# A spectral filter and a gated network on one core: other gates and queues for the opening's loads, two steps' shift of batch 1, and x chunks in whole-width transfers

## The chip, the cores and the metric

The kernel runs on one core of a Trainium2 chip. The metric is the device time of one execution in microseconds (us), the median over the runs; less is better. The profile is of one execution, taken by the hardware profiler. Engines are named as in it: PE is TensorE, DVE is VectorE, ACT is ScalarE, POOL is GpSimd, SP is SyncE. Three of them issue transfers here: SP, ACT and POOL, each in the order of its own program; the profile calls SP's queue q1, ACT's q10 and POOL's q0.

## The reference

`x` has 8 batches of 3008 positions by 256 channels, float32. Each batch is filtered in the frequency domain along its positions, and the result goes through a gated network:

```python
X = np.fft.rfft(x, axis=1)
Y = X * (filt_r + 1j * filt_i)[None, :, :]
y = np.fft.irfft(Y, n=x.shape[1], axis=1)      # (8, 3008, 256)

t = y.reshape(8 * 3008, 256)
gate = np.maximum(t @ w_gate, 0.0)             # (256, 1536)
val = t @ w_val                                # (256, 1536)
out = (gate * val) @ w_out                     # (1536, 256)
```

## The kernel before, in words

A position is written as 32 n1 + n2, with 94 values of n1 and 32 of n2, and the transform of 3008 points is done as matrix products of two levels.

**A** transforms along n1. For batches 0 and 1 this is `first_a` (fp32 products `psA`, evicted by ACT at L289), and `turn_a` on DVE (L301) brings the result into the layout `at`. Batch 0's pieces come first, batch 1's sixteen follow through the iterator `early`. For batches 2 to 7, `load_chunk` brings x in four chunks per batch into the tiles `XP`, `fold_chunk` adds and subtracts them on POOL, `tiled_a` multiplies (`psF`) and stores to `Abuf` in DRAM through SP, and `load_at_tiled` reads `at` back through SP (L355).

**B** has six parts per batch: `fwd` transforms along n2 (`psX`), `product` multiplies with the filters on DVE (`tt`, `uu`), `inv` transforms back (`psD`, evicted into `dsb`) and stores to `Dbuf` in DRAM through SP (L422). Batch 0's last store uses the tile `AS[0][0]` again, which appears as `AS` in `Dbuf<-AS`.

**D** reads `Dbuf` back: `load_d` (L448) makes four tiles `dC` per batch (z = 0 to 3, eight values of n2 each), each with two transfers of 192 KB.

**C** is `item_c`: the last product along n1 for a block of 512 tokens (`psY`, L471), copied to `yT` by ACT for one half and by DVE for the other.

**The network** then takes the 47 blocks of 512 tokens in 12 feature tiles each. `gv` (L487) makes `psV` and `psG`; ACT copies V (`vsb`, L490) and DVE multiplies (`prod`, L492). `o_part` (L508) multiplies the previous block's products with `WoT` and the result goes out through `osb` (L521, L532).

The order of all engines is written out by hand. The opening does A and B of batch 0 with nothing beside them, and the A of batch 1; in between, the last transfers and weights are loaded. After that, one loop over blocks and feature tiles runs, with step number 12 x block + tile. At each step it calls `gv`, then a piece of `o_part`, then whatever `at_step` has put on this step: pieces of A and B of later batches, loads of x and of D. `item_c` for the next block stands at tiles 8 and 10. For batch 1, `end` is step 51; its D is first needed by `item_c` at step 56, where the fifth block runs over from batch 0 into batch 1.

Weights are loaded by POOL, since the transfer also casts to bf16: V and G in two halves each (`load_vg`, the first half has tiles 0 to 5), then `WoT` in two (`load_o`). POOL is kept back by small reads of a tile: `hold_gpsimd` copies eight values of it and so waits until it has been written. POOL's instructions behind such a read wait with it. In the opening, before:

- POOL waits for an eviction of batch 1's A (L274), then issues the first halves of V and G;
- SP issues D's reads for z = 0 and 1, as soon as batch 0's last store has landed;
- POOL waits for the z = 0 tile, then issues the second halves of V and G, `WoT`, and D's reads for z = 2 and 3;
- at step 2, POOL clears the four `XP` tiles (L623), since a chunk's 24-row loads leave rows of 32 unwritten.

The memory of the opening's tiles (the pool `pro`) is given back for the loop's tiles (the pool `fs`).

## Time and profile before

| | us |
|---|---|
| median of 3 runs | 889.26 |
| lowest, highest | 887.65, 892.39 |
| profiled execution, its own time | 888.4 |
| profiled execution, span | 886.3 |
| PE busy | 863.7 (97%) |
| DVE busy | 573.8 (65%) |
| ACT busy | 500.7 (56%) |
| POOL busy | 373.5 (42%) |
| granted TensorE clock, mean | 0.999 |

The span is from the first to the last instruction in the trace; the execution's time has 2.1 us around it. The profile moved 104.41 MB in 105731 packets by DMA, 118 GB/s on average. Matmuls are pipelined, so a busy PE is one with work in it. The waits of PE add up over the whole span; the chain of waits follows the work that ended last back from the end, and says for each piece what released it.

### The profile page before, as it was taken

How to read it: one execution, taken by the hardware profiler on the slowest of the kernel's cores; microseconds unless marked ns; L12 is line 12 of the kernel's file. 1: busy time of each engine (PE TensorE's matmuls, PEld its weight loads, DVE VectorE, ACT ScalarE, POOL GpSimd, SP SyncE). 2: the span in 40 equal slices, each digit the busy share in tenths (PEclk: the TensorE clock that was granted, in tenths of full speed). 3: DMA queues.
4: the chain of work that ended last, by engine and by line, in shares of the span. 5: the costliest groups of instructions: out<-in, count | busy, mean ns of one | idle time of the engine just before them, and what ended most of it. 6: DMA issues, size and time to landing. Idle time of an engine off the chain costs nothing.

```text
span 886.3 us, 19058 instructions
## 1 busy us (share of the span) xinstructions
PE 863.7 (97%) x7071; PEld 508.0 (57%) x7193; DVE 573.8 (65%) x863; ACT 500.7 (56%) x905; POOL 373.5 (42%) x374
## 2 busy tenths in 40 slices
PE   8989999999999999999999999999999999999998
PEld 4336555566556665566655565556655556566665
DVE  3768765577666776667765676657776577655553
ACT  4765554555655565556565556555655555555553
POOL 6661795137641567316771167802867000000001
PEclk9999999999999999999999999999999999999999
DMA  9992466533466337543375234753446512321111
GB/s 238 282 177 49 137 155 139 133 101 113 116 155 137 102 102 165 130 112 101 105 190 131 81 100 129 182 118 84 118 133 150 123 31 81 91 65 36 38 31 54
DMA packets 105731, 104.41 MB, mean 118 GB/s; under 512 B 20215, under 2 KB 90391, under 8 KB 104966
## 3 DMA queue, kind: packets, MB, share of 16 engines
q1 hardware_dynamic: 82374, 75.21, 33.3%
q0 software_dynamic: 22864, 27.19, 13.1%
q8 instruction: 57, 0.93, 0.5%
q10 hardware_dynamic: 400, 0.79, 0.3%
q14 instruction: 36, 0.29, 0.1%
HBM read 58.93 MB, written 46.66 MB: 119 GB/s over the span
## 4 chain that ended last, share of the span: by engine, by line
PE 85%; DMA 7%; DVE 2%; ACT 2%; issue 1%; POOL 1%; SPq 1%; POOLq 0%; DVEq 0%
PE psG L487 26%; PE psO L508 25%; PE psV L487 24%; PE psF L337 3%; PE psD L411 2%; PE psY L471 2%; DVE prod L492 2%; PE psX L374 2%; ACT vsb L490 2%; DMA dC<-Dbuf 2%; DMA at<-Abuf 1%; DMA XF<-in_x_dram 1%; DMA Fti<-in_filt_i_dram 1%; DMA Fti<-Fti 1%; DMA Dbuf<-dsb 1%
## 5 line engine op out<-in xcount | busy, mean ns | idle before, releaser
L492 DVE SCALAR_TENSOR_TENSOR prod<-psG,vsb 128x512 bf16<-128x512 f32 x564 | 388.7, 690 | 259.6 <-ACT vsb L490 253.2
L490 ACT CAST vsb<-psV 128x512 bf16<-128x512 f32 x564 | 331.9, 589 | 265.5 <-PE psV L487 137.4
L508 PE MATMUL psO<-WoT,prod 128*128 128x256 bf16 x2256 | 336.5, 273 | 1.1
L487 PE MATMUL psG<-yT,WgT 128*128 128x512 bf16 x1105 | 330.4, 379 | 5.8 <-DMA WgT<-in_moe_w_gate_dram 0.6
L487 PE MATMUL psV<-yT,WvT 128*128 128x512 bf16 x1031 | 315.9, 380 | 1.2 <-DVE yT L478 0.7
L508 PEld LDWEIGHTS <-prod 128*128 128x128 bf16 x2256 | 220.7, 98 | 143.3
L487 PEld LDWEIGHTS <-WgT 128*128 128x128 bf16 x1128 | 110.0, 98 | 135.6 <-issue 1.8
L487 PEld LDWEIGHTS <-WvT 128*128 128x128 bf16 x1128 | 98.3, 98 | 40.7 <-issue 29.5
L274 POOL CAST scr<-prod 128x8 f32<-128x8 bf16 x24 | 4.5, 190 | 254.7 <-DVE prod L492 254.7
L532 POOL DMA_DIRECT2D out_dram<-osb x5 | 2.6, 535 | 195.7 <-ACT osb L521 195.7
L521 ACT COPY osb<-psO 128x512 f32<-128x512 f32 x92 | 53.9, 586 | 25.8 <-PE psO L508 24.6
L390 DVE TENSOR_TENSOR tt<-psX,Ftr 128x512 bf16<-128x512 f32 x96 | 64.9, 681 | 1.6 <-PE psX L374 0.9
L323 POOL TENSOR_TENSOR fold<-XP 128x1024 f32<-128x1024 f32 x24 | 56.5, 2355 | 19.5 <-PE psF L337 19.3
L390 DVE TENSOR_TENSOR uu<-psX,Fti 128x512 bf16<-128x512 f32 x88 | 59.8, 680 | 0.0
L310 POOL DMA_DIRECT2D XP<-in_x_dram x96 | 56.6, 593 | 2.8 <-PE psY L471 1.4
L324 POOL TENSOR_TENSOR XP<-XP 128x1024 f32<-128x1024 f32 x24 | 56.4, 2349 | 1.9
L419 ACT CAST dsb<-psD 128x512 bf16<-128x512 f32 x94 | 50.6, 592 | 11.0 <-PE psD L411 11.0
L344 ACT CAST asb<-psF 128x512 bf16<-128x512 f32 x48 | 25.8, 589 | 30.1 <-PE psF L337 30.1
L344 DVE CAST asb<-psF 128x512 bf16<-128x512 f32 x48 | 30.9, 686 | 18.1 <-PE psF L337 17.3
L476 ACT CAST yT<-psY 128x512 bf16<-128x512 f32 x47 | 27.5, 586 | 26.1 <-PE psY L471 25.9
L471 PE MATMUL psY<-M,dC 96*128 96x94 bf16 (+18 forms) x604 | 37.7, 198 | 3.6 <-DMA dC<-Dbuf 3.6
L471 PEld LDWEIGHTS <-dC 96*128 96x128 bf16 x604 | 34.4, 97 | 7.9 <-issue 3.4
(73 smaller groups left out, 503.0 us busy)
## 6 DMA issues: line engine op xcount, KB each, us to landing
XP<-in_x_dram POOLq DMA_DIRECT2D x48, 256.0 KB, 6.0
Dbuf<-dsb SPq DMA_DIRECT2D x23, 512.0 KB
dC<-Dbuf SPq DMA_DIRECT2D x60, 192.0 KB
XP<-in_x_dram POOLq DMA_DIRECT2D x96, 96.0 KB, 2.7
Abuf<-asb SPq DMA_DIRECT2D x96, 96.0 KB
at<-Abuf SPq DMA_DIRECT2D x24, 384.0 KB
out_dram<-osb SPq DMA_DIRECT2D x69, 94.0 KB
XF<-in_x_dram SPq DMA_DIRECT2D x20, 256.0 KB
```

The costliest lines, as they stand in the source:

```text
L310: nc.gpsimd.dma_start(xp[r:r + 24, 0:4:2, :], _ap(x, (b * N1 * N2 + o) * D, [[N2 * D, 24], [47 * N2 * D, 2], [1, 512]]))
L323: tt(t, xp[:, 0:2], xp[:, 2:4], op=ALU.add)
L324: tt(xp[:, 2:4], xp[:, 0:2], xp[:, 2:4], op=ALU.subtract)
L344: copy(asf[:, :, q, :], banks[q])
L390: nc.vector.tensor_tensor(p, psX, filt, op=ALU.mult)
L419: copy(dsb[:, a, o:o + 2, :], psD[a])
L471: nc.tensor.matmul(psY[:, o:o + w], dCs[b, n2 // 8][:, n2 % 8, h * 128:(h + 1) * 128], M1[:, n1:n1 + w], start=True, stop=True)
L487: nc.tensor.matmul(pt[:, :W], w[:, h, ft * 128:(ft + 1) * 128], yt[:, h, :], start=(h == 0), stop=(h == 1))
L490: nc.scalar.copy(vsb, psV[:, :W])
L492: nc.vector.scalar_tensor_tensor(prod, in0=psG[:, :W], scalar=0.0, in1=vsb, op0=ALU.max, op1=ALU.mult)
L508: nc.tensor.matmul(psO[:, t % 2], prods[ft][:, t * 128:(t + 1) * 128], WoT[:, ft, :], start=(ft == 0), stop=(ft == NFT - 1))
L521: copy(osb[:, t0 % 2:t % 2 + 1], psO[:, t0 % 2:t % 2 + 1])
```

## The change

- In the opening, six pieces of batch 1's A (three before) stand ahead of the loads. POOL's gate becomes a memset of a few values of `AS[0][0]`, which has to wait until batch 0's last store has read that tile. Behind it, both halves of V and G and `WoT` are issued with no second gate.
- D's read for z = 0 is issued half on SP and half on ACT; z = 1 stays on SP, z = 2 and 3 on POOL.
- The first of the last four `turn_a` pieces of batch 1 moves from step 5 to the end of the opening; the other three go from steps 11, 14, 16 to 6, 12, 14.
- Batch 1's B goes two steps earlier, its D reads one step (50 to 49). The chunks of batch 2 go from steps 22, 29, 34, 43 to 14, 23, 32, 41.
- A chunk is loaded by four transfers of 128 partitions, 256 KB each, in place of four of 96 KB and two of 256 KB; the rows that no product reads now hold other rows of x, and the clearing is gone.

```diff
 def load_chunk(b, j):
     xp = XP[j]
-    for q in range(4):
-        r, o = 32 * q, 8 * q + 2 * j
-        nc.gpsimd.dma_start(xp[r:r + 24, 0:4:2, :],
-                          _ap(x, (b * N1 * N2 + o) * D,
-                              [[N2 * D, 24], [47 * N2 * D, 2], [1, 512]]))
-    for i in range(2):
-        nc.gpsimd.dma_start(xp[:, 2 * i + 1, :],
-                          _ap(x, ((b * N1 + 46 + 47 * i) * N2 + 2 * j) * D,
-                              [[8 * D, 4], [-N2 * D, 32], [1, 512]]))
+    for i in range(4):
+        up = N2 * D if i % 2 == 0 else -N2 * D
+        nc.gpsimd.dma_start(xp[:, i, :],
+                            _ap(x, ((b * N1 + 46 * (i % 2) + 47 * (i // 2)) * N2 + 2 * j) * D,
+                                [[8 * D, 4], [up, 32], [1, 512]]))
...
 first_b(amid)
-for _ in range(3):
-    p, s, h = next(early)
-    first_a(1, p, s, h)
-hold_gpsimd(AS[2][0][:, 4 * s, p, 0:8])
+for _ in range(6):
+    first_a(1, *next(early))
+nc.gpsimd.memset(AS[0][0][:, 0, 0, 0:8], 0.0)
 load_vg(0, DFF // 2)
-load_d(0, 0, 2)
-hold_gpsimd(dCs[0, 0][:, 7, D - 8:])
 load_vg(DFF // 2, DFF)
 load_o()
+load_d(0, 0, 1, (nc.sync, nc.scalar))
+load_d(0, 1, 2)
 load_d(0, 2, 4, (nc.gpsimd, nc.gpsimd))
...
 for h in range(2):
     item_c(0, h)
+turn_a(1, 1, 0, 0, 16)
...
-def clear_chunks():
+def make_chunks():
     for i in range(4):
         XP.append(fs.tile([128, 4, 512], FP32, tag=f"XP{i}", bufs=1, name=f"XP{i}"))
-        nc.gpsimd.memset(XP[i], 0.0)
...
-for k in range(4):
-    at_step((5, 11, 14, 16)[k], lambda k=k: turn_a(1, 1, k // 2, k % 2 * 16, k % 2 * 16 + 16))
-at_step(2, clear_chunks)
+for k in range(1, 4):
+    at_step((6, 12, 14)[k - 1], lambda k=k: turn_a(1, 1, k // 2, k % 2 * 16, k % 2 * 16 + 16))
+at_step(2, make_chunks)
...
-                l = (22, 29, 34, 43)[j] if b == 2 else end - 115 + NFT * j
+                l = (14, 23, 32, 41)[j] if b == 2 else end - 115 + NFT * j
...
-        l = -33 + 5 * i if b == 1 else -40 + 6 * i
+        l = -35 + 5 * i if b == 1 else -40 + 6 * i
...
-    at_step(end - (1 if b == 1 else 2), lambda b=b: load_d(b))
+    at_step(end - 2, lambda b=b: load_d(b))
```

## The prediction

> **What bounds the kernel now.** I read the page first: span, busy time, DMA load over the span.

> ```profile
> span 886.3 us, 19058 instructions
> ...
> PE 863.7 (97%) x7071; PEld 508.0 (57%) x7193; DVE 573.8 (65%) x863; ACT 500.7 (56%) x905; POOL 373.5 (42%) x374
> ...
> DMA  9992466533466337543375234753446512321111
> ```

> TensorE (PE) is busy for 863.7 of 886.3 us, so no scheduling change can win more than 22.6 us, some of it in the first copies and the tail, which this change leaves alone. The DMA digits show where transfers are scarce: the first three slices (66 us), full or nearly. Next, what PE waited for over the whole run.

> ```profile
> PE psY L471 <- DMA dC<-Dbuf: 3.6, 2, 1.9
> ...
> PE psX L374 <- DMA at<-Abuf: 0.8, 1, 0.8
> PE psV L487 <- DVE yT L478: 0.7, 2, 0.4
> PE psG L487 <- DMA WgT<-in_moe_w_gate_dram: 0.6, 1, 0.6
> ```

> Columns: total us, times, longest. The same question for 180 to 800 us returns no row: the steady part has nothing to win. The two psY waits are 1.8 us in the opening and 1.9 us at batch 1's D. The chain of waits shows both, the opening first (start, length, what).

> ```profile
> 40.43 4.99 DMA Dbuf<-AS
> ...
> 45.48 0.33 SPq L448
> ...
> 45.86 6.76 DMA dC<-Dbuf
> ...
> 53.90 6.42 DMA WgT<-in_moe_w_gate_dram
> ...
> 60.37 0.61 PE psG L487 x2
> ```

> D's last store of batch 0 lands at 45.42, its first read at 52.63, and only then do the second halves of V and G leave; PE stops for G's second half until 60.37. The DMA queues between 45.5 and 49.4 us say why the read was slow (queue, packets, MB, share of the 16 engines):

> ```profile
> q0 software_dynamic: 467, 0.69, 108.7%
> ```

> q0 is POOL's queue, with the first halves of V and G. Not one packet of the read, issued on SP (q1) at 45.48, moved in those 3.9 us. From 49.4 to 52.7 us it is the other way:

> ```profile
> q1 hardware_dynamic: 1343, 0.66, 109.1%
> q0 software_dynamic: 57, 0.06, 11.0%
> ```

> POOL's timeline has the issues, and the clearing that goes:

> ```profile
> 43.34 0.78 POOL L262 DMA_DIRECT2D WvT<-in_moe_w_val_dram  x1
> 44.11 0.71 POOL L262 DMA_DIRECT2D WgT<-in_moe_w_gate_dram  x1
> ...
> 58.74 7.09 POOL L623 MEMSET XP<- 128x2048 f32 x4
> ```

> Last, batch 1's D in the chain, and two rows of ACT's timeline:

> ```profile
> 123.09 6.49 DMA Dbuf<-dsb
> ...
> 130.01 6.74 DMA dC<-Dbuf
> ...
> 136.89 0.19 PE psY L471
> ```

> ```profile
> 45.02 0.58 ACT L289 CAST AS<-psA 128x512 bf16<-128x512 f32 x1 [0.27 <-PE psA L282]
> ...
> 51.03 0.65 ACT L289 CAST asb<-psA 128x256 bf16<-128x256 f32 x2 [0.21 <-PE psA L282]
> ```

> **Opening: when D's first read lands.** The memset waits for the store (45.42), then V's issue follows. Before, the hold at 43.10 led to the issue at 43.34, and q0's first packet came at 44.8, 1.4 after the issue. So the first weight packet moves from 44.8 to about 45.5 + 0.2 + 1.4 = 47.1. The read issues at 45.48 on SP; batch 2's read, issued into idle queues at 239.46, starts moving after 1.0 us, so packets flow from 46.5, ahead of the weights. The other half is on ACT, behind the sixth eviction (45.02 + 0.58 = 45.60) and the same store; ACT's issues of x take 0.5 to 0.6 us each and the tail's first one moved packets 0.8 after its issue: 46.4 to 46.7. This issue makes ACT about 0.5 late, and seven evictions are queued behind it; each leaves 0.21 to 0.27 idle and banks are spare, so PE does not see it. In the old run the four 192 KB reads (and WF) took 49.4 to about 54.0, with G's end beside them, some 4.2 us, 0.95 each. Two in front: z = 0 lands at 46.5 + 1.9 + 0.3 = 48.7, before 52.63 and before PE is free. PE's last psA ends at 51.03, so psY starts there, 1.73 us earlier than 52.76; ACT's last eviction (to 51.7), the yT copies (0.6 and 0.7) put psV at 52.4 instead of 53.83.

> **Opening: the weights become late.** Before, they used the DMA engines from 44.8; now these idle until 46.5, and D's reads are first. V's second half was issued at 53.20, G's landed at 60.32: 1.4 to start, about 1.5 extra for ramp and landing, 2.1 for each load. From 46.5: reads 4.2, V and G 4.2 gives 54.9; if the z = 1 reads come later, 53.0. I take 54.7, as the SP issues of z = 1 (46.0 and 46.4, plus 1.0) reach the engines about when V does. So psG starts at 54.7, not 54.38: the 1.8 us wait for dC comes back as a wait for WgT. The second halves now follow without a gap: G's lands at 54.9 + 4.2 = 59.1. Six feature tiles after the first psG took 60.37 - 54.38 - 0.64 = 5.35, so the seventh psG is due at 60.05 and finds its weights: 0.3 earlier than 60.37. With the better order it is 59.1: 1.3 earlier. I take a gain of 0.5. Bounds: all weights in time, 1.4 + 0.64, about 2.1 gained; reads and weights taking turns packet by packet (768 packets of the read at 0.043 us, each behind a weight packet of 0.14, over 16 engines: 8.8 us from 46.7, so z = 0 lands at 55.5 and psG follows at 56.9), 2.5 lost. WoT: 59.1 + 5.5 (its old distance behind G: 65.83 - 60.32) = 64.6; first needed about 66. D's z = 2 and 3 on POOL wait for V and G to land, and are needed after 70.

> DVE's extra transpose (1.21) comes behind yT and ends about 53.9, before the first psG; the piece at step 5 goes to step 6, and one leaves the end of block 0: cost nothing, gain at most the 0.3 us psV wait at 66.22, not counted.

> **Batch 1's D.** B starts two steps earlier. A step is psV, psG, psO: 0.43 + 0.43 + 0.44 = 1.30. The store goes from 123.09 to 120.5, and if store and read keep 6.49 and 6.74, the read lands 2.6 us earlier, at 134.15; PE asked for it at 135.02. The wait of 1.87 is gone even so. Cover on top: the chunk loads, at 121.9 to 125.6 beside this store, move to about 112 (steps 43 to 41, and POOL no longer late by its folds); D's read goes in front of chunk 0's Abuf store (125.99), both on SP, because step 49 lists it first; the Abuf data are not read before 162. Next late is at<-Abuf (0.8 at 176), fed by steps that do not move. Gain 1.9; bounds 0 (if the earlier B work meets DVE at a yT copy and loses as much: that row cost 0.4) and 2.3.

> **Chunks.** Per chunk POOL loses 4 x 0.586 + 2 x 0.702 = 3.75 and gets 4 x 0.702 = 2.81: 22.5 us less over 24 chunks, and 7.1 of memset. No PE row in 180 to 800 waits for POOL or a chunk: worth 0. Bytes rise from 896 to 1024 KB, 3.1 MB of 104.4, where half the DMA time is idle: 0, except at 172 to 176, where a chunk lands beside at<-Abuf: -0.8 to +0.8, taken as 0.

> **Sum.** -0.5 - 1.9 + 0 = -2.4. The profiled run took 888.4 (span 886.3 and 2.1 around it), giving 886.0; the median of the runs shown, 889.26, is 0.9 above it, giving 886.9.

> [...] From 45.5 to 49.4 q0 moved 467 packets and the waiting read none: whoever has work in the engines first keeps them, as far as this row goes. [...] The other: the gap from 51.03 to 52.76, without a busy PE, left the granted clock at 1.00. [...]

> **Rivals.** (1) Slower: the ACT half of the read arrives after the first weight packet (47.1) and, as the read did at 45.5, gets nothing until POOL's queue runs dry: four weights at 2.1 and two WoT loads at 2.75 end at 61.1, the half lands about 62, psY starts 9.3 us late, the G stall of 0.64 and batch 1's 1.9 are saved: +6.8, 896. For: the 3.9 us without a packet. Against: ACT is free at 45.60 and needs to start before about 46.2. Chance 0.10. (2) No gain: the weights' new wait costs 2 and cancels batch 1's gain: 889.3. Chance 0.15. (3) The opening wins its 2.1, batch 1 1.9 and the at wait 0.8: -4.8, 884.5. Against: the DMA digits at 9. Chance 0.15. The forecast has 0.60.

> **Numbers.** 0.5%, about what a measurement of this kernel can tell from no change, is 4.4 us: lines at 884.8 and 893.7. Below 884.8 lie 0.11 of (3) and 0.07 of the forecast (runs spread by 4.7 us): 0.18. Above 893.7: (1) and 0.02 of (2): 0.12. The range, 884.0 to 891.0, takes in (2), (3) and leaves out (1) and the ends.

> **What would show it.** Right: psY near 51.0, psV near 52.4, psG waiting for WgT until 54 to 55, no stall at the seventh psG, no psY wait near 135, at<-Abuf unchanged. Wrong: dC landing after 51, q10 without packets while q0 moves, a granted clock under 1.00 near 55, or new PE rows after 180.

## The result, and the profile after

The changed kernel took 893.06 us (median of 14 runs, 888.30 to 896.10). The kernel before took 888.23 on the same chips (14 runs, 885.38 to 892.39). The ratio, after to before, is 1.0046 with an interval of 1.0028 to 1.0064: slower, by about the size that a measurement of this kernel can tell. The forecast was 886.9, with a range of 884.0 to 891.0 and a chance of 0.12 for more than 893.7: wrong in sign, and 2.1 us above the range. The profiled execution took 893.1 us, 4.7 more than the one before (888.4), so it stands for the difference.

The page of the profile after:

```profile
span 891.3 us, 18890 instructions
...
PE 868.7 (97%) x7072; PEld 510.1 (57%) x7193; DVE 574.0 (64%) x863; ACT 500.6 (56%) x905; POOL 340.6 (38%) x321
...
PEclk9999999989999999999999999999999999999999
...
DMA  9892965746566545573475545764467512331111
```

POOL lost 32.9 us of busy time, more than the 29.6 that the prediction counted, and PE won nothing by it that a row shows. PE is busy for 5.0 us more with the same products. The only row of the page that says why is PEclk: the ninth slice (178 to 200 us) is an 8, where the clock was below full for part of it. PE's waits over the whole run come next (total us, times, longest).

```profile
PE psX L370 <- DMA at<-Abuf: 3.2, 1, 3.2
PE psV L483 <- DMA WvT<-in_moe_w_val_dram: 1.8, 1, 1.8
PE psG L483 <- DMA WgT<-in_moe_w_gate_dram: 1.8, 1, 1.8
...
PE psY L467 <- DMA dC<-Dbuf: 0.5, 1, 0.5
```

Two waits are new, for the first halves of V's and G's weights (before, G's row was 0.6, for the second half). One has grown from 0.8 to 3.2, `at<-Abuf` of batch 2. The wait for `dC` has gone from 3.6 to 0.5: both of its old places are mended (the 0.5 is new, for batch 6's D near 677 us).

The opening in the chain of waits (start, length, what):

```profile
44.92 0.79 POOL WvT L262
45.71 9.53 DMA WgT<-in_moe_w_gate_dram
...
55.29 0.61 PE psG L483
...
56.12 1.06 PE psV L483 x2
57.18 0.85 PE psG L483 x2
...
58.66 0.43 PE psG L483 x2
```

psG waits until 55.29 for G's first half. Behind it, two `psG` take 0.85 where two take 0.43 a little later: PE is at half clock. The busy time of each engine in the two stretches at half clock shows it directly. The columns are the stretch and its length, the busy time and instructions of PE, PEld, DVE, ACT and POOL, the granted clock, the DMA share and GB/s.

```profile
54.88:58.29 3.41, 2.78 (x7) 1.05 (x9) 0.84 (x2) 0.58 (x1) 0.63 (x1) 0.50 1.24 204
177.76:184.59 6.83, 5.93 (x23) 2.77 (x24) 2.79 (x5) 1.17 (x2) 0.00 (x0) 0.50 0.93 118
```

The second stretch holds 23 PE instructions in 6.83 us; the kernel e3 below, with the clock at 1.00, has 41 in 7.00 us at this place. It begins inside the wait for `at`, here in the chain:

```profile
167.01 11.51 DMA at<-Abuf
178.66 0.63 PE psX L370 x5
179.29 0.97 PE psV L483 x2
```

Before, this transfer was issued at 167.54 and took 9.11; now it is issued half a microsecond earlier and takes 11.51. The DMA queues of both kernels say what it met (queue, packets, MB, share of the 16 engines), over 6.5 us that begin 0.46 us behind the first issue of the chunk that lands beside it: first after (172.00 to 178.50), then before (172.52 to 179.02):

```profile
q0 software_dynamic: 531, 0.51, 65.2%
q1 hardware_dynamic: 270, 0.19, 17.3%
```

```profile
q0 software_dynamic: 600, 0.67, 42.0%
q1 hardware_dynamic: 375, 0.27, 17.2%
```

q0 is the first chunk of batch 3, issued at 171.54 (before: 172.06). It moves fewer bytes in this stretch than it did, but its packets hold the engines 1.6 times as long: 0.652 x 16 x 6.5 us for 510 kB is 133 ns of an engine for each kB, where it was 65. (The share adds up the times of packets, and these can overlap: it is 104.4% in a row of e7 below.) q1, with the last of `at` and the outputs, gets 270 packets through and not 375.

Both traces step by step: the start of the first weight load of `psV` at each step, after minus before, with what lies between the rows.

| step | difference, us | what came in between |
|---|---|---|
| 0 | -0.3 | V's first half at 52.91; all of this opening stands 0.4 earlier |
| 1 | +1.1 | psG at 55.29, before 54.38 |
| 3 | +2.4 | half clock, 54.88 to 58.29 |
| 7 | +1.6 | no wait for G's second half |
| 49 | +1.4 | |
| 57 | -0.5 | no wait for batch 1's D |
| 84 | +2.1 | the longer wait for `at` |
| 100 | +4.7 | half clock, 177.76 to 184.59 |
| 417 | +5.4 | the wait for batch 6's D |

So the opening cost 1.6 us where 0.5 was to be won, batch 1's D won the 1.9 forecast for it, and one chunk load, priced at nothing, cost 2.6 by waiting and 2.6 by the clock. Batch 6's D cost another 0.6. Counted from ACT's last eviction of `psA`, which comes 0.4 earlier in this profile, the opening cost 2.0.

### The profile page after: what moved, and what is told of

Same layout as the page of the kernel before. It is cut to its first block, busy times and chain, and to the rows that moved or that the text cites. A ratio compares the mean times of both kernels' runs of the same rounds, so it can differ in the third digit from the quotient of the medians.

```text
span 891.3 us, 18890 instructions
## 1 busy us (share of the span) xinstructions
PE 868.7 (97%) x7072; PEld 510.1 (57%) x7193; DVE 574.0 (64%) x863; ACT 500.6 (56%) x905; POOL 340.6 (38%) x321
## 4 chain that ended last, share of the span: by engine, by line
PE 86%; DMA 5%; DVE 3%; ACT 2%; issue 1%; SPq 1%; POOL 0%; ACTq 0%; DVEq 0%; POOLq 0%
PE psG L483 26%; PE psO L504 26%; PE psV L483 24%; PE psF L333 3%; PE psD L407 2%; PE psY L467 2%; DVE prod L488 2%; ACT vsb L486 2%; PE psX L370 2%; PE psA L282 1%; DMA at<-Abuf 1%; DMA WgT<-in_moe_w_gate_dram 1%; DMA Dbuf<-dsb 1%; DMA XF<-in_x_dram 1%; DVE at L301 1%
## 5 line engine op out<-in xcount | busy, mean ns | idle before, releaser
L517 ACT COPY osb<-psO 128x512 f32<-128x512 f32 x92 | 53.9, 586 | 25.9 <-PE psO L504 22.9
L310 POOL DMA_DIRECT2D XP<-in_x_dram x96 | 64.8, 681 | 0.4 <-issue 0.3
```

The costliest lines, as they stand in the source:

```text
L310: nc.gpsimd.dma_start(xp[:, i, :], _ap(x, ((b * N1 + 46 * (i % 2) + 47 * (i // 2)) * N2 + 2 * j) * D, [[8 * D, 4], [up, 32], [1, 512]]))
L517: copy(osb[:, t0 % 2:t % 2 + 1], psO[:, t0 % 2:t % 2 + 1])
```

## The experiments

The theory after this reading: the loss has two places, the wait for V's and G's first halves and the wait for `at`, and at each the clock adds to the wait. The rivals: POOL, SP and ACT late at other places; the added bytes and not the form of the loads; the slower clock as the cause and not the result. Ratios are of each kernel to the kernel before on the same chip; where a median is compared with another chip's, the ratios are what counts.

**e1_old_loads**: the changed kernel with the old six loads per chunk and the clearing.

```diff
-        for i in range(4):
-            up = N2 * D if i % 2 == 0 else -N2 * D
-            nc.gpsimd.dma_start(xp[:, i, :],
...
+        for q in range(4):
+            r, o = 32 * q, 8 * q + 2 * j
+            nc.gpsimd.dma_start(xp[r:r + 24, 0:4:2, :],
...
+        for i in range(2):
+            nc.gpsimd.dma_start(xp[:, 2 * i + 1, :],
...
+            nc.gpsimd.memset(XP[i], 0.0)
```

> The changed kernel, with the chunk loads of before (four of 96 KB, two of 256 KB, and the clearing) and all else as changed. Theory: the four whole-width loads of batch 3's first chunk (171.5 us) hold the DMA engines from 174 to 183 us in the changed kernel and keep the end of at<-Abuf behind them; PE's wait there is 3.2 us, and the granted clock is halved behind it from 177.8 to 184.6. With the old loads the wait goes back to about 0.8, that half-clock stretch is gone, and the run is about 4.8 us shorter than the changed kernel: 888.3, between 887 and 890. Rival: at<-Abuf is late because batch 1's D read now goes ahead of the Abuf stores on SP; then the wait stays near 3 us and the time near 893.

Measured: 888.75 us, ratio 0.9996 (0.9976 to 1.0016). The wait for `at` is 0.8, as before, and nothing is at half clock near 178; batch 1's D read still goes ahead of the `Abuf` stores on SP, so that order is not what made `at` late. In the opening the two waits (3.1 and 1.9) and one half-clock stretch (56.47, 3.41 us) stay. Without the new loads, what the opening loses and what D wins cancel.

**e2_new_loads**: the kernel before, with the new loads and without the clearing.

```diff
+        for i in range(4):
+            up = N2 * D if i % 2 == 0 else -N2 * D
+            nc.gpsimd.dma_start(xp[:, i, :], ...)
...
-            nc.gpsimd.memset(XP[i], 0.0)
```

> The kernel before, with the whole-width chunk loads and without the clearing, and nothing else of the change. Theory: the wait for at<-Abuf near 177 us grows from 0.8 to about 3 us, half clock follows it, and the run is 3 to 5 us longer than before: 892. Chunk packets take about 300 ns on the mean in place of 230. Rival (SP's order of D read and Abuf stores makes at<-Abuf late): wait 0.8 and time 888, as before.

Measured: 889.86, ratio 1.0012 (0.9991 to 1.0034). The mechanism is there: `at` is waited for 2.6 us, and 3.41 us at half clock begin at 177.66. The size is smaller than expected; the interval takes in both no change and half of the expected loss.

**e3_old_gates**: the changed kernel with the opening of before; steps and loads as changed.

```diff
-    for _ in range(6):
-        first_a(1, *next(early))
-    nc.gpsimd.memset(AS[0][0][:, 0, 0, 0:8], 0.0)
+    for _ in range(3):
+        p, s, h = next(early)
+        first_a(1, p, s, h)
+    hold_gpsimd(AS[2][0][:, 4 * s, p, 0:8])
     load_vg(0, DFF // 2)
+    load_d(0, 0, 2)
+    hold_gpsimd(dCs[0, 0][:, 7, D - 8:])
     load_vg(DFF // 2, DFF)
     load_o()
-    load_d(0, 0, 1, (nc.sync, nc.scalar))
-    load_d(0, 1, 2)
```

> The changed kernel, with the opening's gates and queues of before (first halves of V and G behind an eviction, D's first two reads on SP, second halves behind D's z = 0), all else as changed. Theory: the opening's weights, not its D read, decide in the changed kernel; with the old gates psG starts near 54.2, the seventh psG near 60.3 with its wait of 0.6, no half clock there, and step 49 of the loop starts about 1.5 us earlier than in the changed kernel. The run is 1.5 us shorter than the changed one: 891.5. Rival (the opening is a gain, and all of the loss comes from later): D read lands near 52 again and the run is as long as the changed one or longer by up to 0.5: 893 to 893.6.

Measured: 888.95, ratio 1.0014 (0.9996 to 1.0033). Step 49 comes 2.0 us earlier than in the changed kernel: the price of the new opening in this pair of profiles. It is at the low end. From ACT's last eviction of `psA` to step 7, the five profiles with the old opening (before, e2, e3, e8, f1) take 8.45 to 9.30 us, and the five with the changed opening as it stands (after, e1, e6, e9, g1) 11.25 to 13.28. The wait for `at` is 2.8 us, but in the profiled run it left the clock at 1.00, so that run took 887.65. One and the same wait brings the half clock in one run and not in another.

**e4_filled**: the changed kernel with 17 products of nothing on PE after `turn_a(1,1,0,0,16)`, in the gap before the weights. If the idle time is what halves the clock, this brings it back although the weights come no sooner.

```diff
     turn_a(1, 1, 0, 0, 16)
+    warm(17)
```

> The changed kernel, with 17 matmuls on a constant tile put on PE between the first C products and the first gate product, 3.7 us of PE work without result, in the stretch where PE waits for V's and G's first halves. Theory: the half clock from 54.9 to 58.3 comes from PE's idleness before it; with the filling, psG still starts when G's first half lands, near 55.3, the granted clock is 1.00 there, and step 3 of the loop starts 1.3 to 1.7 us earlier than in the changed kernel; the run is 1.5 us shorter: 891.6. Rival (the clock falls for another reason, such as the load on all engines): half clock stays at 55 to 58 us and the run is 893 or longer.

Measured: 890.15, ratio 1.0018 (0.9997 to 1.0038). The windows at the same two places:

```profile
54.90:58.30 3.40, 2.32 (x11) 1.09 (x12) 1.32 (x2) 1.18 (x3) 0.63 (x1) 1.00 1.25 201
176.92:183.75 6.83, 6.23 (x23) 2.92 (x25) 3.09 (x5) 1.17 (x2) 0.00 (x0) 0.50 0.66 122
```

psG still waits 1.5 us for its weights (to 55.98, 0.7 later than in the changed kernel), yet the clock stays at 1.00: from the first psG to step 7 it takes 5.4 us, and 6.9 in the changed kernel. This profile's opening is no shorter even so, because its weights land later: from the last eviction of `psA` to step 7 both take 11.2. One profile at full clock could be luck, as e3 shows; the runs speak against it, with a mean granted clock of 0.9979 over the 10 of e4 and 0.9947 over the 14 of the changed kernel. The slower clock in the opening thus comes from PE's idle time, and it costs beside the wait that it follows. The second place, untouched, has its stretch as before.

**e6_later_chunk**: the changed kernel with batch 3's first chunk seven steps later, nothing else.

```diff
-                l = (14, 23, 32, 41)[j] if b == 2 else end - 115 + NFT * j
+                l = (14, 23, 32, 41)[j] if b == 2 else end - 115 + NFT * j + (7 if (b, j) == (3, 0) else 0)
```

> The changed kernel, with the first chunk of batch 3 loaded seven steps later (87 in place of 80, about 9 us), all else as changed. Theory: it is the collision of this one chunk with at<-Abuf that costs; the wait near 178 us falls from 3.2 to 0.3 or less, there is no half clock behind it, and the run is 4 to 5 us shorter than the changed one: 888.5. Rival (whole-width loads cost everywhere, through all 24 chunks): the wait moves or shrinks, but the time stays at 891 or more.

Measured: 888.03, ratio 1.0012 (0.9997 to 1.0027). PE's waits from 125 to 880 us are one row; the wait for `at` is gone:

```profile
PE psY L467 <- DMA dC<-Dbuf: 0.3, 1, 0.3
```

The chunk now leaves at 184.43, behind `at`. No stretch at half clock is left near 178. Of 24 chunk loads, this one carries the wait and the half clock of the new form. What the other 23 may cost is in the row above: the 0.3 is for batch 6's D and sets the steps back by 0.5, and neither e1, with the old loads, nor e2, e3 or f1, with the new, has such a wait. What delays this D was not separated.

**e9_same_bytes**: the changed kernel with whole-width loads of 448 of the 512 values of each row, which are the old 896 KB per chunk, with the clearing. It leaves out an eighth of x in batches 2 to 7.

```diff
-            nc.gpsimd.dma_start(xp[:, i, :], ...[1, 512]
+            nc.gpsimd.dma_start(xp[:, i, 0:448], ...[1, 448]
...
+            nc.gpsimd.memset(XP[i], 0.0)
```

> The changed kernel, with whole-width loads of 448 in place of 512 values per row, so that a chunk has the 896 KB of before; an eighth of x is left out for batches 2 to 7 (the clearing stands in for it). Theory A (bytes): with the old bytes, packets and landing go back to the old figures and the wait for at<-Abuf to about 1 us: 889. Theory B (shape: 128 rows at once, all from the first transfer on): the wait stays at 2.5 to 3 us and the time within 1.5 us of the changed kernel's.

Measured: 893.31 (4 runs), ratio 1.0065 (1.0043 to 1.0087), with a wait for `at` of 2.6 and half clock at 55.21 and 178.09. Taking the added bytes away brings back nothing, so the added bytes are not the cause.

**g1_paced**: the changed kernel with a memset of the next quarter on POOL ahead of the second, third and fourth load of each chunk, which spreads the starts of the four issues near `at` from 2.0 to 5.6 us.

```diff
         for i in range(4):
+            if i:
+                nc.gpsimd.memset(xp[:, i, :], 0.0)
```

> The changed kernel, with a memset of the next quarter of the tile on POOL ahead of the second, third and fourth load of each chunk, so that a chunk's four loads are issued over about 4.3 us in place of 2.7. It asks why the same bytes in whole-width loads delay at<-Abuf and the old loads (issued over 3.8 us) do not. Theory A (pace of issue): the wait near 178 us falls from 3.2 to about 1 us. Theory B (shape: whole-width rows on all engines from the first transfer on): the wait stays at 2.5 us or more.

Measured: 890.49, ratio 1.0036 (1.0014 to 1.0059). The wait for `at` is 1.5, between 0.8 and 3.2. Waits of 0.9 and 1.0 for D of batches 5 and 6 cost it another 2.2 in the steps. All kernels that differ in the loads, over the same 6.5 us from 0.46 us behind this chunk's first issue (ns of an engine for each kB worked out as above). That issue stands 4.5 to 4.7 us behind the last issue of `at`, except in e6, where `at` has landed:

| kernel | q0 MB, share of engines | ns per kB | q1 packets | wait for `at` |
|---|---|---|---|---|
| before | 0.67, 42.0% | 65 | 375 | 0.8 |
| e1_old_loads | 0.72, 39.0% | 56 | 336 | 0.8 |
| after | 0.51, 65.2% | 133 | 270 | 3.2 |
| e2_new_loads | 0.68, 64.4% | 98 | 307 | 2.6 |
| e9_same_bytes | 0.68, 62.8% | 96 | 322 | 2.6 |
| g1_paced | 0.63, 42.2% | 70 | 323 | 1.5 |
| e6_later_chunk | 0.94, 63.0% | 70 | 67 | none |

Paced, the same whole-width transfers hold the engines hardly longer for their bytes than the old ones did. Nor do the four of e6, issued in 2.7 us as in the changed kernel but without `at` beside them (74 and 77 ns in f1 and f3, which have e6's line too). So what is slow here is the four at once beside `at`, and neither of the two alone. What keeps the last 0.7 us of the paced kernel's wait was not separated.

**e7_early_halves**: the changed kernel with the first halves of V and G ahead of the store's gate, as before, and the second halves behind it. It tells whether the weights can have their old start beside the new gate.

```diff
-    for _ in range(6):
+    for _ in range(3):
+        p, s, h = next(early)
+        first_a(1, p, s, h)
+    hold_gpsimd(AS[2][0][:, 4 * s, p, 0:8])
+    load_vg(0, DFF // 2)
+    for _ in range(3):
         first_a(1, *next(early))
     nc.gpsimd.memset(AS[0][0][:, 0, 0, 0:8], 0.0)
-    load_vg(0, DFF // 2)
```

> The changed kernel, with the first halves of V and G back behind an eviction (issued near 43.3 us), the second halves and WoT behind D's last store as changed. Theory A (an engine keeps the queue that it serves until it is empty, as from 45.5 to 49.4 us in the kernel before): POOL's queue now has work without a gap, D's first read gets nothing until WoT is in, psY starts after 58 us, and the run is 3 us or more longer than the changed one: 896. Theory B (the queues take turns, as the packets of both queues between 48 and 54 us of the changed kernel suggest): psY starts near 53, psG near 54, the second halves cause no wait, no half clock there, and the run is 2 to 3 us shorter than the changed one: 890.5.

Measured: 891.12 (6 runs), ratio 1.0044 (1.0018 to 1.0069). D's read is issued at 44.3 and moves almost nothing until 48.2; then the queues share. The queues from 44.4 to 48.2 us:

```profile
q0 software_dynamic: 411, 0.61, 104.4%
q1 hardware_dynamic: 1, 0.00, 0.1%
```

and from 49 to 54 us:

```profile
q0 software_dynamic: 474, 0.69, 76.0%
q1 hardware_dynamic: 551, 0.27, 25.7%
q10 hardware_dynamic: 375, 0.18, 12.6%
```

The read lands at 53.77, psY waits 3.6 us, and 6.83 us at half clock begin at 52.8. Neither theory had this order: nothing at all for 3.9 us, and turns after that.

**f2_z1_behind**: the changed kernel with D's z = 1 reads on POOL, behind both halves of V and G and ahead of `WoT`, so that they do not share the engines with the first halves.

```diff
     load_vg(DFF // 2, DFF)
-    load_o()
     load_d(0, 0, 1, (nc.sync, nc.scalar))
-    load_d(0, 1, 2)
+    load_d(0, 1, 2, (nc.gpsimd, nc.gpsimd))
+    load_o()
```

> The changed kernel, with D's z = 1 reads taken from SP and put on POOL behind the four weight loads (ahead of WoT). Theory: the weights are late because D's z = 1 reads and the weights' packets share the engines from 47 to 55 us; without them V's first half lands near 51.5 and G's near 53.3, psG starts 1.5 to 2 us earlier than in the changed kernel, the half clock near 55 is seldom, and the run is 2 to 3.5 us shorter than the changed one: 890. Rival (the weights are late only because they are issued late, and take their time alone): psG still near 55, time as the changed kernel, 893.

Measured: 891.08, ratio 1.0034 (1.0017 to 1.0050). psG comes 3.91 us after psY's start, where the changed kernel has 4.85: 0.95 won, less than expected. The waits for V and G shrink from 1.8 to 1.4 and 1.3, and are still waits; this profile has no half clock in the opening. **f3_z1_behind_later** is the same with e6's line:

> The kernel of the last experiment (D's z = 1 behind the weights) with batch 3's first chunk seven steps later as well: both stalls of the changed kernel are then treated, and its gain at batch 1's D remains. If both theories hold, no wait over 1 us remains behind 55 us, the granted clock is 1.00 after the first 60 us, and it is faster than before by 2 us: 885. Rival (half clock in the opening stays, or z = 1 comes too late for the second block): 887 to 889.

Measured: 885.34, ratio 0.9982 (0.9965 to 0.9998), as expected in size. The opening is not cured: the same order as f2 here waits 2.4 and 0.8 us for V and G, and 6.83 us at half clock begin at 53.11.

**e8_steps_only**: the kernel before with only the new steps for `turn_a`, batch 2's chunks, batch 1's B and its D.

```diff
+    turn_a(1, 1, 0, 0, 16)
...
-    for k in range(4):
-        at_step((5, 11, 14, 16)[k], ...)
+    for k in range(1, 4):
+        at_step((6, 12, 14)[k - 1], ...)
...
-                l = (22, 29, 34, 43)[j] if b == 2 else end - 115 + NFT * j
+                l = (14, 23, 32, 41)[j] if b == 2 else end - 115 + NFT * j
...
-            l = -33 + 5 * i if b == 1 else -40 + 6 * i
+            l = -35 + 5 * i if b == 1 else -40 + 6 * i
...
-        at_step(end - (1 if b == 1 else 2), lambda b=b: load_d(b))
+        at_step(end - 2, lambda b=b: load_d(b))
```

> The kernel before, with only the new steps: batch 1's B two steps earlier, its D read at step 49, the four transposes and batch 2's chunks at their new steps; old gates, old queues, old loads with the clearing. Theory: the wait of 1.9 us for batch 1's D is gone, the wait for at<-Abuf stays at 0.8, nothing else changes: 2 us shorter than before, 885.5 (ratio 0.998). Rival (the earlier steps give the gain back, at the yT copies or at at<-Abuf): same as before, 887.4.

Measured: 885.41, ratio 0.9977 (0.9962 to 0.9992): 2.0 us won, with no wait near 135. **f1_steps_loads_later** adds to it the new loads without the clearing, and e6's line: everything but the opening.

> The kernel before with the new steps, the whole-width loads without clearing, and batch 3's first chunk seven steps later; the old gates and queues. Theory: whole-width loads cost nothing once that collision is away, so the time is that of the new steps alone, 885.4 (ratio to before 0.998), with the clearing gone. Rival (whole-width loads cost in all chunks): 886.5 or more, and later waits appear behind 180 us.

Measured: 884.04 (881.86 to 888.28), ratio 0.9960 (0.9944 to 0.9977), by its ratio faster than both kernels. Its waits from 55 to 880 us, all of them:

```profile
PE psV L483 <- DVE yT L474: 0.6, 2, 0.4
PE psG L483 <- DMA WgT<-in_moe_w_gate_dram: 0.5, 1, 0.5
PE psV L483 <- issue: 0.2, 1, 0.2
```

f3 and f1 differ in the opening alone. The new opening, even with f2's better order, is 885.34 and the old one 884.04 on the same chip; the intervals of the two ratios overlap.

## Why the prediction was wrong, point by point

**Opening: when D's first read lands.** Right. psY starts at 50.44 with no wait for `dC` (forecast 51.03; the span's start makes up some 0.4 of that). The first rival, ACT's half starved for 9.3 us, did not come: the read was issued at 44.39 and 44.80, ahead of V's weights at 44.92.

**Opening: the weights become late.** Here is the first step that failed. G's first half was put at 54.7 and landed for 55.29, 0.6 off; V's was taken as in time for 52.4 and was there at 52.91, a wait that the working did not have. The mis-sized figure is the weights' start: POOL issued V at 44.92, 0.8 earlier than the working had it, but its first packet moved 2.6 after the issue and not 1.4. From 44.92 to 47.50 q1 moved 623 packets and q10 392, the reads of D, and q0 none. The seventh psG found its weights, as forecast. By these alone the opening would have been psG's 0.9 us later, less the 0.8 of the second halves' wait: a loss of 0.1 (0.5 with the 0.4 by which this opening stands earlier) in place of the gain of 0.5. The other 1.5 of the measured +1.6 are the clock. The prediction's sum has no term for the clock; the row that it had on it is one gap of 1.73 us in the old trace (51.03 to 52.76), which left the clock at 1.00. Here PE has one pair of products between 51.07 and 55.29, two waits of 1.8 us that come one after the other. A single gap of the same length was not the nearest row for that. In e4, with the time before psV filled and a wait of 1.5 for G left, the clock stayed at 1.00.

In the traces every stretch at half clock behind a wait is 3.41 or 6.83 us; the changed kernel has one of each. Its stretches at full clock behind them are whole multiples of the shorter one, taken as 3.413: 119.47 us is 35 times that, 706.56 is 207 times. The traces also show what goes ahead of a halving, if each is cut into pieces of 3.41 us on its own grid. These are the pieces ahead of the two stretches in the changed kernel, and then the two over which e3's wait of 2.8 us falls (columns as above; the second figure is PE's busy time):

```profile
51.47:54.88 3.41, 0.60 (x2) 0.11 (x2) 1.42 (x2) 0.90 (x2) 0.64 (x1) 1.00 1.16 214
174.35:177.76 3.41, 1.11 (x9) 0.50 (x6) 1.12 (x2) 1.17 (x2) 0.00 (x0) 1.00 0.96 116
```

```profile
172.06:175.48 3.42, 1.79 (x17) 0.89 (x14) 1.79 (x3) 1.17 (x2) 0.58 (x1) 1.00 0.89 124
175.48:178.89 3.41, 2.23 (x17) 1.26 (x18) 1.32 (x3) 0.59 (x1) 0.00 (x0) 1.00 1.03 187
```

PE is idle for 2.8 and 2.3 us of the first two, and half clock follows; for 1.6 and 1.2 of e3's, and it does not. Over all 14 profiles, up to 860 us, the 12 pieces at full clock in which PE idles for 2.08 us or more are all followed by half clock, and no piece with 1.76 or less is; of the three between (1.86 to 1.87) one is. So a wait that falls across two pieces can leave neither idle enough, which is e3 (2.8 us, clock 1.00) against e4 (2.8 us, with 2.2 idle in one piece, and half clock for 6.83 us). The gap of 1.73 us that the prediction went by lay in a piece with 1.5 idle.

**Batch 1's D.** Right. Its store was issued at 121.75 (before 123.09), the read at 129.80 on SP in front of the chunk's `Abuf` store at 133.84, and no row of PE is left near 135. The term of -1.9 measured -1.9 in the steps and -2.0 as e8.

**Chunks.** The second step that failed: "worth 0", and for `at<-Abuf` -0.8 to +0.8. POOL's saved 32.9 us were indeed worth nothing. The prediction had also named the right place, a chunk landing beside `at` at 172 to 176, and took 14% more bytes as the measure of what could change there. e9 shows that the bytes are not it. The form, beside `at`, is: four transfers issued in 2.7 us double the engines' time for each kB (65 to 133 ns), and a wait of 0.8 becomes 3.2. The clock again adds to that: 2.6 us behind 2.6. Nothing had been allowed for the clock here, because the bound of the wait was itself under a microsecond.

**The sum.** Forecast: -0.5 - 1.9 + 0. Measured, by the steps: +1.4 at step 49, then -1.9 + 2.6 + 2.6 + 0.6, which with rounding is the +5.4 of step 417; in the tail 0.4 of it comes back (the spans differ by 5.0). Of this, 1.5 + 2.6 are the clock. Over all runs it is somewhat less: the mean granted clock is 0.9947 over the 14 runs of after, and 0.9980 over the 31 runs of the kernel before on e1's chip; 0.0033 x 890 is, as an estimate, 2.9 us of the 4.8 between the medians. In the one run of after that kept a clock of 0.999, it took 888.3, as much as the kernel before. That the clock follows the waits, and not the other way, is e4, e6 and f1: where the wait or the idle time went, the stretch at that place went with it. The forecast also started from the median of 3 runs, 889.26, which is 1.0 above that of 14.

**Turns packet by packet.** The prediction had them as a bound, and went by the row with 467 packets against none. A read kept out and queues that share were both seen, one after the other: e7's reads moved 1 packet against 411 in 3.8 us, and from 49 to 54 us q1 and q10 moved 551 and 375 beside 474 of q0. In what order the packets take turns, no row shows. In the changed kernel, D's z = 1 and `WF` share the engines with V and G between 48 and 54 us (606 packets of q0, 541 of q1), which f2 undid, to win 0.95 us. In the prediction's bound with turn-taking, the loss was 2.5; the opening lost 1.6, most of it for another reason.

**Rivals.** The second, that the weights' wait of 2 cancels batch 1's gain, describes the opening and D together: e1 gives it, at 0.9996. No rival joined two waits and the clock, and slower than 891 was left almost wholly to the one mechanism that did not come.

## What to carry to other kernels

When a change moves waits, add up the time in which TensorE is nearly idle around each of them, short work between two waits included, and price at least 3.41 us at half clock behind it where they can put 2 us or more of idle time into one piece of 3.41, as in all 12 such pieces here; a single short gap that cost nothing is no proof. When a transfer's form changes at equal bytes, look at which other transfer is in flight beside it at each place where it runs, and shift that one issue instead of judging the form: here one chunk of 24, seven steps later, turned a loss into part of the best version. Parts of a change are worth trying alone: the new steps won 2.0 us by themselves, and the opening that came with them was better left as it was.
